# Second MLP product of a token-mixing block: five of seven block products take both parts of their moving operand in one 512-column matmul

## The chip, the cores and the metric

The kernel runs on one core of a Trainium2 chip. The metric is the device time of one execution in microseconds (us). Every time below that carries a position, such as "at 393.73", counts from the start of the profiled span.

## The reference, cut to what matters

Two blocks follow one another on an array x of 2048 tokens by 512 channels: linear attention with a residual, then an MLP over the token axis with a residual. All is float32.

```python
h = x + _A_ref(_layernorm(x), A_wqkv, A_w_phi, A_wo)
# _B_ref on layernorm(h), h here normalised once more:
u = jnp.einsum("bsd,sf->bdf", h, w1) + b1     # f = 1792
u = _gelu(u)
y = jnp.einsum("bdf,fs->bds", u, w2) + b2     # s = 2048
out = h + y transposed to (tokens, channels)
```

The change concerns only the last product, y = u w2.

## The kernel before, in words

**Split products.** Every large product is taken in three matmuls on rounded numbers. An operand is split in a high part (rounded, made by ScalarE) and a low part (the rest, made by VectorE or GpSimd), and the matmuls are high by high, high by low and low by high, summed in PSUM. `split` (L56 to L59) does this: L58 is the ScalarE copy, L59 the subtraction.

**The second MLP product.** The output is made in eight pairs of 128-row blocks (`sp` = 0 to 7), the contraction over f in seven pairs of 128 (`p` = 0 to 6). For each (sp, p) there is a 2 by 2 block product with 256 by 256 blocks of columns, and it is computed in Strassen-Winograd's way: seven block products instead of eight, on sums of blocks of w2 (stationary) and of u (moving). `STEPS` (L775) lists the 56 steps. A stationary block is 128 by 128, a moving block 128 by 256 (`HD`), with its high and low part lying side by side in one tile (`UB[p, m]`, 128 by 2 by 256). So a step is 7 products of 3 matmuls of 256 columns, 21 matmuls (`product`, L799 to L801). All seven sums of a pair of row blocks fit in four PSUM banks of 2 by 256 columns; two sums share a bank. Pairs with even sp take the four banks of pool `ps_b`, pairs with odd sp the two of `ps_f` and the two of `ps_q`, eight banks in all (L818, L819).

**Preparing w2.** `stream_w2` (L779 to L793) prepares two steps at a time, called a group here. It loads the blocks (L785, SyncE's DMA queue), forms three sums and replaces one block by a difference (L789 to L792, VectorE, 128 by 256 each), and splits the 128 by 1792 result (L793, which calls L58 on ScalarE into `whi` and L59 on VectorE into `wlo`). `whi` and `wlo` have two buffers each and `wraw` three, so the split of group g+1 begins when TensorE is done with group g-1. A pair of row blocks is seven steps, so its end falls in the middle of a group after even sp, and on the end of a group after odd sp.

**Closing a pair.** At p = 6 the products are issued bank by bank (L825, L830). Then (L832 to L839) ScalarE copies one sum to SBUF (`e`), VectorE forms `u2`, `u3` and the second `e` from banks and SBUF, and two VectorE operations of 512 columns add the bias and the remaining banks into `ot`. GpSimd's queue then sends two DMAs that add `ot` to the output in memory (L839), where the residual already stands. The last pair (L842 to L859) instead loads its rows of the output to `hb`, collects the last three steps bank by bank, and adds everything there on VectorE.

**What sets the order.** From L709 on, no order is written by hand: a list scheduler with its own estimates of durations fixes the order on each engine at build time. It takes the ready instruction that was traced first. So TensorE's order can differ from the loop's: where a low part is late by the scheduler's estimate, matmuls with high parts are put ahead. On the chip each engine follows the fixed order and waits where it must. A bank counts as one thing: VectorE and ScalarE read it only after all traced matmuls into it.

Of the kernel before, what the change touches and what calls it, by code (L numbers as in the profile page):

```python
# [9 lines left out]
F32 = mybir.dt.float32  # L10
F32R = mybir.dt.float32r
AF = mybir.ActivationFunctionType
ALU = mybir.AluOpType
# [4 lines left out]
P = 128  # L18
# [16 lines left out]
def block_kernel(ctx: ExitStack, tc: tile.TileContext, x, xT, wT, phic, wo, w1, b1, w2, b2,  # L35
                 kvmask, ident_in, out):
    nc = tc.nc
# [9 lines left out]
    b2s = cst.tile([P, NT], F32, name="b2s")  # L47
# [8 lines left out]
    def split(hi, lo, src, lo_engine):  # L56

        nc.scalar.activation(hi, src, AF.Copy)  # L58
        lo_engine.tensor_sub(lo, src, hi)  # L59
# [9 lines left out]
    ps_q = ctx.enter_context(tc.tile_pool(name="ps_q", bufs=2, space=PSUM, side="right"))  # L69
# [28 lines left out]
    def load_x(t):  # L98
        raw = kk.tile([P, KD, P], F32, name="xraw", bufs=3)
        nc.sync.dma_start(raw, xT[t])  # L100
        return raw
# [298 lines left out]
    for t in range(3, NT - 1):  # L400
        if t + 2 < NT:
            raw = load_x(t + 2)
# [108 lines left out]
    ps_f = ctx.enter_context(tc.tile_pool(name="ps_f", bufs=2, space=PSUM, reuse_waits="tile"))  # L511
# [210 lines left out]
    NP = NF // 2  # L722
    HD = D // 2
    up = ctx.enter_context(tc.tile_pool(name="up", bufs=1, side="right", reuse_waits="tile"))
    uo = ctx.enter_context(tc.tile_pool(name="uo", bufs=2, side="right", reuse_waits="tile"))
    ws = ctx.enter_context(tc.tile_pool(name="ws", bufs=2, side="right", reuse_waits="tile"))
    ur = ctx.enter_context(tc.tile_pool(name="ur", bufs=4, side="right", reuse_waits="tile"))
    ut = ctx.enter_context(tc.tile_pool(name="ut", bufs=1, side="right", reuse_waits="tile"))
    ps_b = ctx.enter_context(tc.tile_pool(name="ps_b", bufs=4, space=PSUM, reuse_waits="tile"))
# [3 lines left out]
    U, UB, far = {}, {}, {}  # L733
# [39 lines left out]
    hp = ctx.enter_context(tc.tile_pool(name="hp", bufs=1, reuse_waits="tile"))  # L773

    STEPS = [(sp, p) for sp in range(NT // 2) for p in range(NP)]  # L775
    GRP = 2
    AW = {}

    def stream_w2(n):  # L779
        steps = STEPS[n:n + GRP]  # L780
        raw = ws.tile([P, GRP, 7, P], F32, name="wraw", bufs=3)
        wh_ = ws.tile([P, GRP, 7, P], F32R, name="whi")
        wl_ = ws.tile([P, GRP, 7, P], F32R, name="wlo")
        for i, (sp, p) in enumerate(steps):
            nc.sync.dma_start(raw[:, i, 0:4].rearrange("p (k i) s -> p k (i s)", k=2),  # L785
                              w2v[:, 2 * p:2 * p + 2, sp * 2 * P:(sp + 1) * 2 * P])
            AW[sp, p] = wh_[:, i], wl_[:, i]
        with tc.issue_after(LO[-18]):
            nc.vector.tensor_add(raw[:, :, 4], raw[:, :, 0], raw[:, :, 2])  # L789
            nc.vector.tensor_sub(raw[:, :, 0], raw[:, :, 1], raw[:, :, 0])  # L790
            nc.vector.tensor_sub(raw[:, :, 5], raw[:, :, 4], raw[:, :, 1])
            nc.vector.tensor_sub(raw[:, :, 6], raw[:, :, 3], raw[:, :, 5])  # L792
        split(wh_, wl_, raw, nc.vector)  # L793


    PROD = ((1, 1, 0, 0, True), (2, 6, 2, 1, True), (3, 3, 3, 1, True), (4, 4, 2, 0, False), (0, 0, 1, 0, True),
            (5, 5, 0, 1, False), (6, 2, 3, 0, False))

    def product(o, a, b, start, stop):  # L799
        for i, (x, y) in enumerate(((0, 0), (0, 1), (1, 0))):  # L800
            nc.tensor.matmul(o, a[x], b[:, y], start=start and i == 0, stop=stop and i == 2, skip_group_check=True)  # L801

    def products(sp, ps, order):
        for a, b, bk, half, opens in order:
            for p in ps:
                wh_, wl_ = AW[sp, p]
                product(bank[bk][:, half], (wh_[:, a], wl_[:, a]), UB[p, b], p == 0 and opens, p == NP - 1)

    def flat(a):
        return a.rearrange("p k d -> p (k d)")  # L810

    for n, (sp, p) in enumerate(STEPS):
        t = 2 * sp
        last = t + 2 == NT
        if n % GRP == 0:
            stream_w2(n)
        if p == 0:
            pools = [ps_f, ps_f, ps_q, ps_q] if sp % 2 else [ps_b] * 4  # L818
            bank = [pool.tile([P, 2, HD], F32, name="py", tag="pu") for pool in pools]  # L819
        if p < NP - 1 - 2 * last:  # L820
            products(sp, [p], PROD)
            continue
        if p < NP - 1:
            continue
        by_bank = sorted(PROD, key=lambda m: m[2:4])  # L825
        e = uo.tile([P, 2, HD], F32, name="e")
        u2 = uo.tile([P, HD], F32, name="u2", bufs=1)
        u3 = uo.tile([P, HD], F32, name="u3")
        if not last:
            products(sp, [p], by_bank)  # L830
            ot = uo.tile([P, 2, 2, HD], F32, name="ot", bufs=1)
            nc.scalar.activation(e[:, 1], bank[0][:, 0], AF.Copy)  # L832
            nc.vector.tensor_add(u2, bank[0][:, 1], e[:, 1])
            nc.vector.tensor_add(u3, bank[1][:, 0], u2)
            nc.vector.tensor_add(e[:, 0], bank[2][:, 0], u2)
            for i, add in enumerate((u3.unsqueeze(1).to_broadcast([P, 2, HD]), e)):
                nc.vector.scalar_tensor_tensor(ot[:, i], bank[2 + i], b2s[:, t + i:t + i + 1], add,  # L837
                                               op0=ALU.add, op1=ALU.add)
                nc.gpsimd.dma_start(out[(t + i) * P:(t + i + 1) * P, :], flat(ot[:, i]), accum_op=ALU.add)  # L839
            continue  # L840

        hb = [hp.tile([P, 2, HD], F32, name=f"hb{i}") for i in range(2)]  # L842
        for i in range(2):
            nc.sync.dma_start(flat(hb[i]), out[(t + i) * P:(t + i + 1) * P, :])
            nc.vector.tensor_scalar(hb[i], hb[i], b2s[:, t + i:t + i + 1], None, op0=ALU.add)
        products(sp, [p - 2, p - 1, p], by_bank)
        nc.scalar.activation(e[:, 1], bank[0][:, 0], AF.Copy)
        nc.vector.tensor_add(hb[1][:, 1], bank[0][:, 0], hb[1][:, 1])
        nc.vector.tensor_add(u2, bank[0][:, 1], e[:, 1])
        nc.vector.tensor_add(hb[1][:, 0], u2, hb[1][:, 0])  # L850
        nc.vector.tensor_add(u3, bank[1][:, 0], u2)
        nc.vector.tensor_add(hb[0], hb[0], u3.unsqueeze(1).to_broadcast([P, 2, HD]))
        nc.vector.tensor_add(hb[0][:, 0], bank[2][:, 0], hb[0][:, 0])
        nc.vector.tensor_add(hb[1][:, 0], bank[2][:, 0], hb[1][:, 0])
        nc.vector.tensor_add(hb[0][:, 1], bank[2][:, 1], hb[0][:, 1])
        nc.sync.dma_start(out[t * P:(t + 1) * P, :], flat(hb[0]))
        for k, q in ((0, nc.scalar), (1, nc.sync)):
            nc.vector.tensor_add(hb[1][:, k], bank[3][:, k], hb[1][:, k])
            q.dma_start(out[(t + 1) * P:NT * P, k * HD:(k + 1) * HD], hb[1][:, k])  # L859
# [47 lines left out]
```

## Time and profile before

| what | value |
|---|---|
| median of 3 runs | 526.02 us (525.8 to 526.22) |
| profiled execution, its own time | 526.04 us |
| its span in the trace | 524.3 us |
| second MLP product: first and last matmul start | 378.62 and 519.61 us |
| TensorE busy over the span | 517.7 us, 4000 matmuls |
| VectorE busy | 384.5 us, 681 instructions |
| ScalarE busy | 277.8 us, 475 instructions |
| GpSimd busy | 229.4 us, 174 instructions |

Rows of the profile name a group by the kernel's line, the engine (PE is TensorE, PEld its weight loads, DVE VectorE, ACT ScalarE, POOL GpSimd, SP SyncE), the operation, and the tiles as output<-inputs with their shape. After the bar come the busy time and the mean of one in ns, then the idle time of the engine before these instructions with what ended it. In a timeline the first column is the start, the second how long the row lasts; rows of one kind that follow one another are merged ("x8"). Matmuls are pipelined, so the duration of one (283 ns for 256 columns) is longer than the distance between two starts, and it is the distance that counts.

### The profile page before, as it was taken

How to read it: one execution, taken by the hardware profiler on the slowest of the kernel's cores; microseconds unless marked ns; L12 is line 12 of the kernel's file. 1: busy time of each engine (PE TensorE's matmuls, PEld its weight loads, DVE VectorE, ACT ScalarE, POOL GpSimd, SP SyncE). 2: the span in 40 equal slices, each digit the busy share in tenths (PEclk: the TensorE clock that was granted, in tenths of full speed). 3: DMA queues.
4: the chain of work that ended last, by engine and by line, in shares of the span. 5: the costliest groups of instructions: out<-in, count | busy, mean ns of one | idle time of the engine just before them, and what ended most of it. 6: DMA issues, size and time to landing. Idle time of an engine off the chain costs nothing.

```text
span 524.3 us, 10150 instructions
## 1 busy us (share of the span) xinstructions
PE 517.7 (99%) x4000; PEld 446.6 (85%) x4000; DVE 384.5 (73%) x681; ACT 277.8 (53%) x475; POOL 229.4 (44%) x174
## 2 busy tenths in 40 slices
PE   8999999999999999999999999999999999999996
PEld 7888888887877777777788888888899999999996
DVE  6893999986997899697336425726668878888774
ACT  6999853434267877767756433426544333343330
POOL 2579698985989999974224000000001101101110
PEclk9999999999999999999999999999999999999999
DMA  8643210021303333333255432532015556535631
GB/s 304 198 132 121 75 47 22 1 83 60 103 21 101 102 101 108 115 101 123 81 173 154 115 101 81 181 102 80 20 41 122 144 139 154 126 123 133 150 71 50
DMA packets 45487, 55.85 MB, mean 107 GB/s; under 512 B 3968, under 2 KB 33024, under 8 KB 45440
## 3 DMA queue, kind: packets, MB, share of 16 engines
q1 hardware_dynamic: 43136, 51.38, 30.9%
q0 software_dynamic: 2016, 3.67, 5.3%
q8 instruction: 31, 0.51, 0.4%
q10 hardware_dynamic: 288, 0.17, 0.1%
q14 instruction: 16, 0.13, 0.1%
HBM read 46.81 MB, written 8.39 MB: 105 GB/s over the span
## 4 chain that ended last, share of the span: by engine, by line
PE 95%; DVE 3%; ACT 1%; issue 0%; DVEq 0%; ACTq 0%
PE py L801 26%; PE pu L63 13%; PE pu L64 12%; PE pu L65 12%; PE pv L64 3%; PE pv L65 3%; PE po L63 3%; PE pv L63 3%; PE po L65 3%; PE po L64 3%; PE pk_ps L63 2%; PE pk_ps L65 2%; PE pk_ps L64 2%; PE pn L549 2%; PE tr L531 2%; PE kvp L208 2%
## 5 line engine op out<-in xcount | busy, mean ns | idle before, releaser
L839 POOL DMA_DIRECT2D out<-ot x14 | 12.4, 996 | 210.9 <-DVE ot L837 210.9
L801 PE MATMUL py<-uf,whi 128*128 128x256 f32 x560 | 96.2, 283 | 0.0
L58 ACT ACTIVATE whi<-wraw 128x1792 fp32r<-128x1792 f32 x28 | 47.7, 1704 | 77.9 <-PE py L801 73.8
L63 PE MATMUL pu<-hs,whi 128*128 128x512 f32 x224 | 87.7, 394 | 0.0
L64 PE MATMUL pu<-hs,whi 128*128 128x512 f32 x224 | 87.2, 389 | 0.0
L65 PE MATMUL pu<-hs,wlo 128*128 128x512 f32 x224 | 86.7, 389 | 0.0
L801 PEld LDWEIGHTS py<-uf,whi 128*128 128x128 f32 x560 | 83.3, 192 | 0.0
L610 DVE TENSOR_TENSOR wlo<-wraw,whi 128x512 fp32r<-128x512 f32 x56 | 47.3, 847 | 44.7 <-ACT whi L603 44.5
L59 DVE TENSOR_TENSOR wlo<-wraw,whi 128x1792 fp32r<-128x1792 f32 x28 | 56.6, 2022 | 18.6 <-ACT whi L58 18.6
L801 PE MATMUL py<-uf,wlo 128*128 128x256 f32 x280 | 69.9, 283 | 0.0
L603 ACT ACTIVATE whi<-wraw 128x512 fp32r<-128x512 f32 x56 | 34.6, 625 | 45.0 <-PE pu L64 40.8
L63 PEld LDWEIGHTS pu<-hs,whi 128*128 128x128 f32 x224 | 42.0, 188 | 9.1 <-ACT hj L581 0.2
L801 PEld LDWEIGHTS py<-uf,wlo 128*128 128x128 f32 x280 | 49.7, 192 | 0.0
L65 PEld LDWEIGHTS pu<-hs,wlo 128*128 128x128 f32 x224 | 42.0, 188 | 8.9
L64 PEld LDWEIGHTS pu<-hs,whi 128*128 128x128 f32 x224 | 42.1, 188 | 8.5
L443 POOL TENSOR_TENSOR ez<-eq,zB 128x1024 f32<-128x1024 f32 x16 | 38.5, 2408 | 4.4 <-ACT zB L487 4.4
L801 PE MATMUL py<-un,whi 128*128 128x256 f32 x224 | 38.4, 283 | 0.0
L196 POOL TENSOR_TENSOR pk<-pk,sk 128x1024 f32<-128x1024 f32 x16 | 31.0, 1941 | 7.7 <-DVE sk L195 5.4
L467 POOL TENSOR_TENSOR eq<-eq,w 128x1024 f32<-128x1024 f32 x16 | 32.4, 2025 | 3.2 <-DVE w L464 3.2
L801 PEld LDWEIGHTS py<-un,whi 128*128 128x128 f32 x224 | 33.2, 192 | 0.1
L200 POOL TENSOR_TENSOR zacc<-zacc,pk 128x1024 f32<-128x1024 f32 x13 | 31.2, 2404 | 0.5
L172 ACT ACTIVATE pk<-pk,r 128x1024 f32<-128x1024 f32 x16 | 18.4, 1147 | 17.9 <-DVE pk L150 17.7
(172 smaller groups left out, 1174.6 us busy)
## 6 DMA issues: line engine op xcount, KB each, us to landing
wraw<-in_w SPq DMA_DIRECT2D x112, 256.0 KB, 2.9
xraw<-in_xT SPq DMA_DIRECT2D x16, 256.0 KB, 3.1
xh<-in_x SPq DMA_DIRECT2D x16, 256.0 KB, 2.6
h<-in_x SPq DMA_DIRECT2D x16, 256.0 KB, 2.7
out<-h SPq DMA_DIRECT2D x16, 256.0 KB, 2.0
out<-ot POOLq DMA_DIRECT2D x14, 256.0 KB, 4.7
wraw<-in_wT SPq DMA_DIRECT2D x12, 256.0 KB, 5.1
wo<-in_wo SPq DMA_DIRECT2D x4, 256.0 KB, 3.8
```

The costliest lines, as they stand in the source:

```text
L58: nc.scalar.activation(hi, src, AF.Copy)
L59: lo_engine.tensor_sub(lo, src, hi)
L63: nc.tensor.matmul(o, ah, bh, start=first, stop=False)
L64: nc.tensor.matmul(o, ah, bl, start=False, stop=False)
L65: nc.tensor.matmul(o, al, bh, start=False, stop=last)
L196: nc.gpsimd.tensor_mul(heads(PK[t]), heads(PK[t]), sk.unsqueeze(2).to_broadcast([P, 2 * H, DH]))
L200: nc.gpsimd.tensor_add(zacc, zacc, PK[t])
L443: nc.gpsimd.tensor_mul(EZ[t], EQ[t], zB)
L467: nc.gpsimd.tensor_mul(heads(EQ[t]), heads(EQ[t]), W[t].rearrange("p g c h -> p (g c h)").unsqueeze(2).to_broadcast([P, 2 * H, DH]))
L603: nc.scalar.activation(wh_, raw, AF.Copy)
L610: LO.append(nc.vector.tensor_sub(wl_, raw, wh_).ins)
L801: nc.tensor.matmul(o, a[x], b[:, y], start=start and i == 0, stop=stop and i == 2, skip_group_check=True)
```

## The change

For pairs sp = 0 to 6, five of the seven products become "wide": one matmul of 512 columns takes the high stationary part against high and low moving part at once, and a second one of 256 columns takes the low stationary part against the high moving part. The 512 results are a full bank: the high sums in one half, the low sums in the other. These five products have a bank each (`b3`, `b2`, `b7`, `b5`, `b4`). The other two (P1 and P6) stay as they were and share `b16`. A pair now takes six banks: `b3` and `b2` come from `ps_f` and `ps_q` in turn, and `b16`, `b7`, `b5`, `b4` are the four banks of `ps_b` in every pair. At p = 0 to 5 the order is b3, b2, then b16, b7, b5, b4; at p = 6 it is b16, b7, b5, b4, then b3, b2.

Closing a pair now has six ScalarE copies of 256 columns (the `e` of before and the five low halves into `low`), seven VectorE operations of 256 columns (three as before, and four in the place of two of 512), and four GpSimd additions (three of 512 columns, one of 256) that bring `low` into `ot` before each DMA. `in_order` ties these ScalarE and VectorE operations to one order within each engine.

The last pair keeps its 21 narrow matmuls per step, in an order by bank at all p, and takes its four banks from `ps_b`. The split of w2 does the low part in two VectorE operations of 896 columns, one per step. The last group's `whi` and `wlo` get buffers of their own.

```diff
+        end = n + GRP == len(STEPS)
+        wh_ = (hp if end else ws).tile([P, GRP, 7, P], F32R, name="whi")
+        wl_ = (hp if end else ws).tile([P, GRP, 7, P], F32R, name="wlo")
...
-        split(wh_, wl_, raw, nc.vector)
+        nc.scalar.activation(wh_, raw, AF.Copy)
+        for i in range(GRP):
+            nc.vector.tensor_sub(wl_[:, i], raw[:, i], wh_[:, i])
...
+    P1, P2, P3, P4, P5, P6, P7 = (1, 1), (3, 3), (6, 2), (2, 6), (4, 4), (5, 5), (0, 0)
+
+    def narrow(o, ps, m, sp, opens, closes):
+        for p in ps:
+            wh_, wl_ = AW[sp, p]
+            for i, (x, y) in enumerate(((wh_, 0), (wh_, 1), (wl_, 0))):
+                nc.tensor.matmul(o, x[:, m[0]], UB[p, m[1]][:, y], start=opens and p == 0 and i == 0,
+                                 stop=closes and p == NP - 1 and i == 2, skip_group_check=True)
+
+    def wide(o, p, m, sp):
+        wh_, wl_ = AW[sp, p]
+        nc.tensor.matmul(o, wh_[:, m[0]], UB[p, m[1]], start=p == 0, stop=False, skip_group_check=True)
+        nc.tensor.matmul(o[:, 0], wl_[:, m[0]], UB[p, m[1]][:, 0], start=False, stop=p == NP - 1, skip_group_check=True)
+
+    def in_order(*groups):
+        at = {}
+        for op in [op for group in groups for op in group]:
+            with ExitStack() as st:
+                for ins in at.values():
+                    st.enter_context(tc.issue_after(ins))
+                ins = op().ins
+            at[ins.engine] = ins
...
+        if not last:
+            if p == 0:
+                b3, b2 = [new_bank((ps_f, ps_q)[sp % 2]) for _ in range(2)]
+                b16, b7, b5, b4 = [new_bank(ps_b) for _ in range(4)]
+            first, second = ([lambda: wide(b3, p, P3, sp), lambda: wide(b2, p, P2, sp)],
+                             [lambda: narrow(b16[:, 0], [p], P1, sp, True, True),
+                              lambda: narrow(b16[:, 1], [p], P6, sp, False, True),
+                              lambda: wide(b7, p, P7, sp), lambda: wide(b5, p, P5, sp), lambda: wide(b4, p, P4, sp)])
+            for f in second + first if p == NP - 1 else first + second:
+                f()
...
+            low = hp.tile([P, 5, HD], F32, name="low")
+            copies = [lambda: nc.scalar.activation(e[:, 1], b16[:, 0], AF.Copy)]
+            for i, o in ((0, b5), (4, b7), (1, b4), (2, b3), (3, b2)):
+                copies.append(lambda i=i, o=o: nc.scalar.activation(low[:, i], o[:, 1], AF.Copy))
+            adds = [lambda: nc.vector.tensor_add(u2, b16[:, 1], e[:, 1]),
+                    lambda: nc.vector.tensor_add(u3, b7[:, 0], u2),
+                    lambda: nc.vector.tensor_add(e[:, 0], b5[:, 0], u2)]
+            for i, k, o, add in ((0, 0, b5, u3), (0, 1, b4, u3), (1, 0, b3, e[:, 0]), (1, 1, b2, e[:, 1])):
+                adds.append(lambda i=i, k=k, o=o, add=add: nc.vector.scalar_tensor_tensor(
+                    ot[:, i, k], o[:, 0], b2s[:, t + i:t + i + 1], add, op0=ALU.add, op1=ALU.add))
+            in_order(copies[:1] + adds[:1], adds[1:2], copies[1:4], adds[2:5], copies[4:], adds[5:])
+            nc.gpsimd.tensor_add(ot[:, 0], ot[:, 0], low[:, 0:2])
+            nc.gpsimd.tensor_add(ot[:, 0], ot[:, 0], low[:, 4:5].to_broadcast([P, 2, HD]))
+            nc.gpsimd.dma_start(out[t * P:(t + 1) * P, :], flat(ot[:, 0]), accum_op=ALU.add)
+            nc.gpsimd.tensor_add(ot[:, 1], ot[:, 1], low[:, 2:4])
+            nc.gpsimd.tensor_add(ot[:, 1, 0], ot[:, 1, 0], low[:, 0])
+            nc.gpsimd.dma_start(out[(t + 1) * P:(t + 2) * P, :], flat(ot[:, 1]), accum_op=ALU.add)
+            continue
         if p == 0:
-            pools = [ps_f, ps_f, ps_q, ps_q] if sp % 2 else [ps_b] * 4
+            b16, b7, b54, b32 = [new_bank(ps_b) for _ in range(4)]
...
+        if p < NP - 3:
+            for o, m, opens in places:
+                narrow(o, [p], m, sp, opens, True)
```

More of the change, by code (lines that the diff above doesn't have):

```diff
@@ L781, in stream_w2 @@
         raw = ws.tile([P, GRP, 7, P], F32, name="wraw", bufs=3)
-        wh_ = ws.tile([P, GRP, 7, P], F32R, name="whi")
-        wl_ = ws.tile([P, GRP, 7, P], F32R, name="wlo")
+        end = n + GRP == len(STEPS)
+        wh_ = (hp if end else ws).tile([P, GRP, 7, P], F32R, name="whi")
+        wl_ = (hp if end else ws).tile([P, GRP, 7, P], F32R, name="wlo")
         for i, (sp, p) in enumerate(steps):
@@ L792, in stream_w2, with new_bank @@
             nc.vector.tensor_sub(raw[:, :, 6], raw[:, :, 3], raw[:, :, 5])
-        split(wh_, wl_, raw, nc.vector)
[L796 to L807, printed above, removed]
+        nc.scalar.activation(wh_, raw, AF.Copy)
[20 more added lines that the diff above has]
+            at[ins.engine] = ins
     def flat(a):
         return a.rearrange("p k d -> p (k d)")
+    def new_bank(pool):
+        return pool.tile([P, 2, HD], F32, name="py", tag="pu")
     for n, (sp, p) in enumerate(STEPS):
@@ L816, in block_kernel @@
             stream_w2(n)
-        if p == 0:
-            pools = [ps_f, ps_f, ps_q, ps_q] if sp % 2 else [ps_b] * 4
-            bank = [pool.tile([P, 2, HD], F32, name="py", tag="pu") for pool in pools]
-        if p < NP - 1 - 2 * last:
-            products(sp, [p], PROD)
+        if not last:
[8 more added lines that the diff above has]
+                f()
+            if p < NP - 1:
+                continue
+            e = uo.tile([P, 2, HD], F32, name="e")
+            u2 = uo.tile([P, HD], F32, name="u2", bufs=1)
+            u3 = uo.tile([P, HD], F32, name="u3")
+            ot = uo.tile([P, 2, 2, HD], F32, name="ot", bufs=1)
+            low = hp.tile([P, 5, HD], F32, name="low")
[15 more added lines that the diff above has]
+            nc.gpsimd.dma_start(out[(t + 1) * P:(t + 2) * P, :], flat(ot[:, 1]), accum_op=ALU.add)
+            continue
@@ L822, in block_kernel @@
+        if p == 0:
+            b16, b7, b54, b32 = [new_bank(ps_b) for _ in range(4)]
+            places = ((b16[:, 0], P1, True), (b16[:, 1], P6, False), (b7[:, 0], P7, True), (b54[:, 0], P5, True),
+                      (b54[:, 1], P4, False), (b32[:, 0], P3, True), (b32[:, 1], P2, False))
+        if p < NP - 3:
+            for o, m, opens in places:
+                narrow(o, [p], m, sp, opens, True)
             continue
         if p < NP - 1:
-            continue
-        by_bank = sorted(PROD, key=lambda m: m[2:4])
@@ L826, in block_kernel @@
[L826 to L839, printed above, removed]
@@ L845, in block_kernel @@
             nc.vector.tensor_scalar(hb[i], hb[i], b2s[:, t + i:t + i + 1], None, op0=ALU.add)
-        products(sp, [p - 2, p - 1, p], by_bank)
+        for o, m, opens in places:
+            narrow(o, [p - 2, p - 1, p], m, sp, opens, True)
+        bank = b16, b7, b54, b32
+        e = uo.tile([P, 2, HD], F32, name="e")
+        u2 = uo.tile([P, HD], F32, name="u2", bufs=1)
+        u3 = uo.tile([P, HD], F32, name="u3")
         nc.scalar.activation(e[:, 1], bank[0][:, 0], AF.Copy)
```

## The prediction

> **What bounds the kernel now.** I read the chain that ended last first, then the matmul starts in the timeline, then the groups and the stage table, and last the waits.
>
> The chain, in order of time; its last rows:
>
> ```profile
> 378.78 137.53 PE py L801 x1146
> 516.33 0.39 ACT e L847
> ...
> 520.55 0.33 DVE hb L858
> ```
>
> The second MLP product is one unbroken run of matmuls. From 516.33 on, the chain leaves TensorE: the closing of the last pair hangs on one ScalarE copy and the VectorE additions behind it. The granted clock is 1.00 in every stretch that I asked for.
>
> The price of a matmul is the distance between starts, at 512 columns (first MLP product) and at 256:
>
> ```profile
> 309.71 0.39 PE L65 MATMUL pu<-hs,wlo 128*128 128x512 f32 x1
> ...
> 317.87 0.39 PE L65 MATMUL pu<-hs,wlo 128*128 128x512 f32 x1
> 380.29 0.28 PE L801 MATMUL py<-un,wlo 128*128 128x256 f32 x1
> 380.41 0.40 PE L801 MATMUL py<-un,whi 128*128 128x256 f32 x2
> 380.65 0.28 PE L801 MATMUL py<-un,wlo 128*128 128x256 f32 x1
> ```
>
> Between the first two rows lie 36 starts: 8.16/36 = 0.2267 us each. The narrow ones start 0.12 apart, and the whole product agrees: (519.61 - 378.62)/1175 = 0.1200. So there is no hole in it, and twice the columns cost 0.1067 more: a matmul is 0.1067 us per 256 columns plus 13.3 ns fixed.
>
> VectorE is the second engine. Groups, and the stage table for 400 to 500 (columns after the stretch: length, then busy time of PE, PEld, DVE, ACT, POOL):
>
> ```profile
> L59 DVE TENSOR_TENSOR wlo<-wraw,whi 128x1792 fp32r<-128x1792 f32 x28 | 56.6, 2022 | 18.6 <-ACT whi L58 18.6
> L790 DVE TENSOR_TENSOR wraw<-wraw 128x256 f32<-128x256 f32 x28 | 11.8, 421 | 0.6
> L837 DVE SCALAR_TENSOR_TENSOR ot<-py,b2s,u 128x512 f32<-128x512 f32 x7 | 5.2, 742 | 0.0
> 400.00:420.00 20.00, 20.00 (x169) 20.00 (x168) 17.45 (x27) 7.04 (x6) 3.69 (x4) 1.00 0.61 129
> 420.00:440.00 20.00, 20.00 (x169) 20.00 (x168) 16.04 (x25) 7.05 (x6) 1.74 (x2) 1.00 0.49 129
> ```
>
> With 15.60, 16.23 and 16.98 in the next three stretches VectorE is busy 82.3 of 100 us, or 14.5 of the 17.64 us (147 x 0.12) of a pair of row blocks. GpSimd does next to nothing here. That changes.
>
> **1. Matmuls: -3.27 us.** A wide product replaces three narrow matmuls (0.360) by one of 512 and one of 256 (0.2267 + 0.12 = 0.3467). Five per step: 0.0667 us; 7 steps in 7 pairs: 49 x 0.0667 = 3.27 us, all on the path. A pair then takes 7 x (5 x 0.3467 + 6 x 0.12) = 17.17 us. The bounds are 0 (a 512 matmul costs two of 256) and 3.27; I take 3.27, the row of 512 being the very form.
>
> [...]
>
> **2. The end: -0.2 us.** Before, the `whi` of the last group waits for a buffer, so the first bank of the last pair closes at 516.3, and ten VectorE operations in a row reach to 520.88. With its own buffers that split can come earlier and the bank closes sooner. What is late next is the last bank: its last matmul starts at 519.61, and a reader starts some 0.3 later, 519.9 instead of L858's 520.13. Bounds 0 and 0.4 (an earlier DMA of the first rows); I take 0.2.
>
> **3. VectorE and GpSimd: 0 to +2.0 us, taken +0.6.** Per pair VectorE has 14 operations L789 to L792, 7 halves of `wlo` (896 columns; between 0.69 us for 512, L610, and 2.02 for 1792: 1.09) and 7 closing operations of 0.42: 5.88 + 7.63 + 2.94 = 16.45 us. Queued ones start 0.33 apart where they last 0.42 (413.33, 413.66), so 28 x 0.08 comes off: 14.2 us packed tight. New are four GpSimd additions per pair: 512 columns with two full inputs are 1.30 us (L59 on POOL), 256 are 0.74 (L745): 4.64 us. They cost VectorE something:
>
> ```profile
> 227.80 1.94 POOL L467 TENSOR_TENSOR eq<-eq,w 128x1024 f32<-128x1024 f32 x1 [1.86 <-DVE w L464]
> 228.19 2.10 DVE L610 TENSOR_TENSOR wlo<-wraw,whi 128x512 fp32r<-128x512 f32 x1
> 234.77 1.94 POOL L467 TENSOR_TENSOR eq<-eq,w 128x1024 f32<-128x1024 f32 x1 [0.43 <-DVE w L464]
> 235.22 2.03 DVE L610 TENSOR_TENSOR wlo<-wraw,whi 128x512 fp32r<-128x512 f32 x1
> ```
>
> An L610 lasts 0.69 alone. Started under a GpSimd operation it ends 0.55 and 0.54 us after that one's end (229.74 to 230.29, 236.71 to 237.25): it stood still until then. L789 to L792 and `wlo` read two SBUF tiles as L610 does; closing operations read a bank. So a pair's additions can hold VectorE for 4.64, less 0.84 for the two closing operations that run beside the first, less 4 x 0.14 (0.69 - 0.55) that passes in the shadow: 3.2 us. 14.2 + 3.2 = 17.4, 0.28 over TensorE's 17.17: +2.0 us in seven pairs if nothing of it falls in idle time. But VectorE idles 3.1 us a pair now, mostly for `whi` (18.6 in L59's row), and part falls there: I take 0.6, nearer to zero. The extra five ScalarE copies (0.385 each, L832) meet an engine that is busy 7 of 20 us. GpSimd has 4.64 us and two DMA issues of 1.0 us in 17: its DMAs land some 5 us later, before `ot` is wanted again.
>
> [...]
>
> **4. Banks: 0 to +6.1 us, taken +1.0.** Before, a pair had four banks that the next did not touch. Now `ps_b` serves every pair, so the next pair's first matmul into `b16` waits for `u2` (its reader), which waits for `e`. Call T the start of step p = 6. TensorE reaches the new `b16` at T + 2.45 (the step) + 0.69 (the new b3 and b2) = T + 3.15. In the trace of before, after an even pair:
>
> ```profile
> 395.55 2.02 DVE L59 TENSOR_TENSOR wlo<-wraw,whi 128x1792 fp32r<-128x1792 f32 x1 [1.42 <-ACT whi L58]
> 395.85 0.38 ACT L832 ACTIVATE e<-py 128x256 f32<-128x256 f32 x1 [0.34 <-PE py L801]
> 397.82 0.42 DVE L833 TENSOR_TENSOR u<-py,e 128x256 f32<-128x256 f32 x1
> ```
>
> T is 393.73; `u2` stands behind a whole `wlo` and ends at 398.24, T + 4.51, 1.36 us too late. After an odd pair it ends at 413.41 with T = 411.37, T + 2.04: in time. Queued behind a waiting b16 matmul is everything on TensorE, unless the scheduler has put the b3 and b2 products of the group's further steps ahead: four wide ones, 1.39 us, just the cover. Halved, `wlo` lets `u2` in 0.93 us earlier. The last pair has no b3 and b2 of its own: its first matmul is due at T + 2.45, so 2.06 us late at before's offsets, some 1.1 with the halves. Upper bound 3 x 1.36 + 2.06 = 6.1; lower bound 0, all covered. I take 0.1 for each of three even pairs and 0.7 for the last: 1.0.
>
> **The sum**, against the profiled execution's own 526.04 (span 524.3 and 1.7 around it; the median is 526.02): 526.04 - 3.27 - 0.2 + 0.6 + 1.0 = 524.2 us.
>
> **Rivals.**
> - *VectorE becomes the bound, and the kernel is slower.* Its work of a pair is then not 14.2 but half way to the 15.3 that today's busy time gives (14.5 + 0.56 for the halves + 0.2 for four closing operations), 14.8, and the whole 3.2 of GpSimd's additions lies on it: 18.0 per pair against 17.64 before. +0.36 x 7 = 2.5, + 1.0 - 0.2: 529.3 us. It decides from 2.8 us held per pair. For it: the four rows above and the backlog of `wlo` just behind a closing. Against it: 3.1 us of idle time.
> - *The banks eat the gain.* Half of the upper bound of step 4, 3.05: 526.04 - 3.47 + 0.6 + 3.05 = 526.2 us. For it: `u2` behind `wlo` in every even pair. Against it: the cover of 1.39.
> - *The 512 matmul saves nothing here*, the fixed 13.3 ns going with each half bank written: 526.04 - 0.2 + 1.6 = 527.4 us. Against it: the 512-column rows write whole banks at 226.7.
>
> **Chances.** The forecast's case 0.56, VectorE 0.21, banks 0.18, no saving 0.05. A measurement can tell about 0.2%, 1.05 us, from no change. Faster: 0.53 of the first and 0.03 of the banks' case, 0.56. Within: 0.03 and 0.10, 0.13. Slower: 0.21, 0.05 of banks, 0.05: 0.31. The forecast's own range is 522.3 (no waits, the end's 0.4) to 525.5. To hold 8 in 10 it has to reach over the banks and half of VectorE's case: 522.3 to 529.3.
>
> **What would show it.** Step 1: wide starts 0.227 and 0.120 apart, a pair of 17.17 us. Step 2: the last pair's `e` copy well before the last bank. Step 3: `wlo` halves of over 1.1 us under a GpSimd addition, and weight loads or matmuls with `wlo` that wait for VectorE. Step 4: idle time before the first b16 matmul of a pair, largest before the last pair. I am wrong if pairs take over 17.64 us, by whichever of these waits.

## The result, and the profile after

The changed kernel takes **554.48 us** (553.44 to 556.48, 6 runs) against 526.13 (525.8 to 526.39, 6 runs with the three above): ratio 1.0545, 95% interval 1.0521 to 1.0569. That is 5.4% slower, 25 us above the top of the predicted range. The profiled execution has a span of 551.7 us, 27.4 more than before. The second MLP product alone went from 141.0 to 169.4 us between its first and last matmul start, 28.4 more; the first MLP product and what lies before it end within 0.4 us of where they ended. All ratios are of undisturbed executions; one execution of the kernel of experiment 6 took 1018.94 us, with TensorE busy for 1011.5 us on its 3755 matmuls (515.3 in experiment 12), for a cause that stays open, and is left out.

Groups of the changed kernel's page. L812 and L813 are the 512-column and the 256-column matmul of a wide product, L796 a half of `wlo`, L790 the first of the four operations on `wraw`:

```profile
L796 DVE TENSOR_TENSOR wlo<-wraw,whi 128x896 fp32r<-128x896 f32 x56 | 61.7, 1152 | 8.8 <-ACT whi L794 8.8
L812 PE MATMUL py<-uf,whi 128*128 128x512 f32 x175 | 57.0, 400 | 5.9 <-ACT whi L794 5.9
L813 PE MATMUL py<-uf,wlo 128*128 128x256 f32 x175 | 37.9, 286 | 7.3 <-DVE wlo L796 7.2
L790 DVE TENSOR_TENSOR wraw<-wraw 128x256 f32<-128x256 f32 x28 | 15.1, 546 | 22.3 <-DMA wraw<-in_w 22.1
```

TensorE, which never waited in this product before, now does, for three things (all its waits in this stage):

```profile
PE py L813 <- DVE wlo L796: 9.1, 9, 1.4
PE py L812 <- ACT whi L794: 5.9, 6, 1.0
PE py L806 <- DVE u L857: 5.4, 6, 3.5
```

These count idle time only. Measured as the distance between two starts beyond 120 ns (256 columns) or 227 ns (512), it is 11.6 us at low parts, 6.9 at high parts and 6.3 at banks that `u2` has yet to read. Of the 31.6 us by which the starts lie further apart than these pitches, that is 24.8; the half clock below takes 2.8, and the rest is in delays of under 0.2 us and in the pitch of the wide matmuls. A pair shows the first two waits behind its closing; timeline of TensorE, then of GpSimd, VectorE and ScalarE in the same stretch:

```profile
403.06 0.28 PE L813 MATMUL py<-uf,wlo 128*128 128x256 f32 x1
404.29 0.73 PE L812 MATMUL py<-uf,whi 128*128 128x512 f32 x2 [0.96 <-ACT whi L794]
...
405.10 0.86 PE L812 MATMUL py<-uf,whi 128*128 128x512 f32 x3
407.35 0.51 PE L813 MATMUL py<-uf,wlo 128*128 128x256 f32 x2 [1.40 <-DVE wlo L796]
```

```profile
402.64 1.39 POOL L867 TENSOR_TENSOR ot<-ot,low 128x512 f32<-128x512 f32 x1 [1.15 <-DVE ot L861]
404.00 1.48 POOL L865 TENSOR_TENSOR ot<-ot,low 128x512 f32<-128x512 f32 x1
402.82 1.50 DVE L792 TENSOR_TENSOR wraw<-wraw 128x256 f32<-128x256 f32 x1
404.36 1.41 DVE L793 TENSOR_TENSOR wraw<-wraw 128x256 f32<-128x256 f32 x1
402.54 3.29 ACT L794 ACTIVATE whi<-wraw 128x1792 fp32r<-128x1792 f32 x2 [2.61 <-PE py L812]
```

L792 and L793 last 0.42 us alone; here they take 1.50 and 1.41 us and end some 0.3 us after a GpSimd addition does (404.32 after 404.03, 405.77 after 405.48), and the `wlo` behind them starts 1.4 us after `whi` was there. ScalarE makes two `whi` in one go: both buffers came free at nearly the same time.

VectorE's waits for the loads of w2 grow too, from 8.0 to 21.2 us in this product, but they are not the price: experiment 12 below still has 17.4 us of them and takes no longer than the kernel before.

The largest single hole (a stretch in which TensorE idles) stands before the last pair, and the clock falls behind it (timeline of TensorE, then the stage table, whose third column from the right is the granted clock):

```profile
522.87 0.76 PE L813 MATMUL py<-uf,wlo 128*128 128x256 f32 x5
527.15 0.80 PE L806 MATMUL py<-un,whi 128*128 128x256 f32 x2 [3.52 <-DVE u L857]
```

```profile
528.00:534.00 6.00, 6.00 (x32) 6.00 (x32) 5.37 (x9) 2.79 (x5) 4.37 (x3) 0.56 0.01 3
534.00:540.00 6.00, 6.00 (x51) 5.94 (x50) 3.28 (x3) 1.71 (x1) 3.49 (x4) 1.00 0.52 70
```

Up to 533.5 the narrow matmuls start 214 ns apart instead of 120: 2.8 us more, on top of the hole's 3.7.

### The profile page after: what moved, and what is told of

It reads as the page before. It is cut to its first block, busy times and chain, and to the rows that moved or that the text cites. A ratio compares the mean times of both kernels' runs of the same rounds, so it can differ in the third digit from the quotient of the medians.

```text
span 551.7 us, 9807 instructions
## 1 busy us (share of the span) xinstructions
PE 524.7 (95%) x3755; PEld 434.4 (79%) x3755; DVE 407.9 (74%) x723; ACT 287.5 (52%) x510; POOL 265.2 (48%) x202
## 5 line engine op out<-in xcount | busy, mean ns | idle before, releaser
L864 POOL TENSOR_TENSOR ot<-ot,low 128x512 f32<-128x512 f32 x7 | 9.0, 1287 | 201.0 <-DVE ot L861 201.0
L796 DVE TENSOR_TENSOR wlo<-wraw,whi 128x896 fp32r<-128x896 f32 x56 | 61.7, 1152 | 8.8 <-ACT whi L794 8.8
L812 PE MATMUL py<-uf,whi 128*128 128x512 f32 x175 | 57.0, 400 | 5.9 <-ACT whi L794 5.9
L813 PE MATMUL py<-uf,wlo 128*128 128x256 f32 x175 | 37.9, 286 | 7.3 <-DVE wlo L796 7.2
L806 PE MATMUL py<-uf,whi 128*128 128x256 f32 x210 | 40.7, 285 | 0.0
L813 PEld LDWEIGHTS py<-uf,wlo 128*128 128x128 f32 x175 | 29.0, 190 | 12.1 <-DVE wlo L796 10.8
L812 PEld LDWEIGHTS py<-uf,whi 128*128 128x128 f32 x175 | 29.6, 189 | 11.1 <-ACT whi L794 7.8
L806 PEld LDWEIGHTS py<-uf,whi 128*128 128x128 f32 x210 | 34.4, 194 | 2.3
L790 DVE TENSOR_TENSOR wraw<-wraw 128x256 f32<-128x256 f32 x28 | 15.1, 546 | 22.3 <-DMA wraw<-in_w 22.1
```

Of the source, the lines that this page charges most:

```text
L796: nc.vector.tensor_sub(wl_[:, i], raw[:, i], wh_[:, i])
L806: nc.tensor.matmul(o, x[:, m[0]], UB[p, m[1]][:, y], start=opens and p == 0 and i == 0, stop=closes and p == NP - 1 and i == 2, skip_group ...
L812: nc.tensor.matmul(o, wh_[:, m[0]], UB[p, m[1]], start=p == 0, stop=False, skip_group_check=True)
L813: nc.tensor.matmul(o[:, 0], wl_[:, m[0]], UB[p, m[1]][:, 0], start=False, stop=p == NP - 1, skip_group_check=True)
```

## The experiments

Three theories are named in what was expected. A hand-over is the step from one pair's closing to the next pair's first use of the same banks. **L**: GpSimd's additions hold VectorE, so `wlo` comes late. **B**: two buffers of `whi` and `wlo` are too few once TensorE runs products of later steps early, since both then stay in use and the next split starts late. **S**: sharing `ps_b` between pairs is the price.

**1. The changed kernel without GpSimd's additions**

```diff
-            nc.gpsimd.tensor_add(ot[:, 0], ot[:, 0], low[:, 0:2])
-            nc.gpsimd.tensor_add(ot[:, 0], ot[:, 0], low[:, 4:5].to_broadcast([P, 2, HD]))
...
-            nc.gpsimd.tensor_add(ot[:, 1], ot[:, 1], low[:, 2:4])
-            nc.gpsimd.tensor_add(ot[:, 1, 0], ot[:, 1, 0], low[:, 0])
```

> The changed kernel without its four GpSimd additions per pair; the low sums of the wide products are copied to SBUF but left out of the output. The order on TensorE is the same for the first half of the product. Theory L (the additions hold VectorE, so wlo comes late): VectorE gets back some 3.4 us per pair, the wlo waits of TensorE (9 to 13 us in all) go, and the time falls below 542. Theory B (products pulled ahead keep both whi/wlo buffers taken, so the next split starts too late): whi waits of about 1.1 us per pair stay, the time stays above 545.

Measured: 535.58 us, ratio to before 1.019 (1.0175 to 1.0205), 18.9 us less than the changed kernel. The waits for `wlo` fall from 11.6 to 0.4 us, measured as distances, and the other losses fall with them: waits for `whi` from 6.9 to 5.1, for `u2` from 6.3 to 3.3, the loss at half clock from 2.8 to 1.5 (granted clock 0.91 from 500 to 520). The waits that are left, in idle time:

```profile
PE py L812 <- ACT whi L794: 4.2, 6, 1.0
PE py L806 <- DVE u L857: 2.8, 3, 2.5
```

The operations on `wraw` are back at 0.42 us each. Over the product VectorE's L790 to L793 and L796 take 21.3 us less, 3.0 per pair, so the hold itself was predicted well (3.2). L is right for the largest part; most of the `whi` waits stay, as B says, though the time fell far below B's 545.

**2. A third pair of `whi` and `wlo` tiles**

```diff
-        end = n + GRP == len(STEPS)
+        end = n > 0 and n // GRP % 3 == 0
```

> The changed kernel with a third whi and wlo buffer (every third group takes the pair of tiles that only the last group had). Theory B: the split of the next group no longer waits for TensorE; whi and wlo waits go and the time falls below 535. Theory L: VectorE is held as before, so at most the whi waits (7 us) go: about 547.

Measured: 548.16 us, 1.0413 (1.0377 to 1.0449), 6.3 us less than the changed kernel. In its profiled execution (544.46 us, the fastest of four) no wait for `whi` is left; those for `wlo` are 9.0 us and for `u2` 7.4. That is near L's forecast for this edit, and it sizes B's part.

**3. The kernel before with one set of banks**

```diff
-            pools = [ps_f, ps_f, ps_q, ps_q] if sp % 2 else [ps_b] * 4
+            pools = [ps_b] * 4
```

> The kernel before with one edit: every pair takes the four banks of ps_b. No wide products, no additions. Theory S (sharing banks between pairs is the price): at least +1.5 us per hand-over, over 535. Theories L and B: TensorE's work is unchanged and little is late, 526 to 531.

Measured: 546.13 us, 1.0392 (1.0368 to 1.0416). Sharing alone, with no wide matmul and no addition, costs 20 us, far beyond the 6.1 that the prediction held for the most. The first hand-over in its timeline:

```profile
395.14 2.02 DVE L59 TENSOR_TENSOR wlo<-wraw,whi 128x1792 fp32r<-128x1792 f32 x1 [1.43 <-ACT whi L58]
395.73 0.28 PE L801 MATMUL py<-uf,wlo 128*128 128x256 f32 x1
397.42 0.42 DVE L833 TENSOR_TENSOR u<-py,e 128x256 f32<-128x256 f32 x1
397.89 0.73 PE L801 MATMUL py<-un,whi 128*128 128x256 f32 x2 [1.89 <-DVE u L833]
```

It is the picture of step 4: `u2` stands behind a whole `wlo`, here with no b3 and b2 to cover it. The seven waits for `u2` are 10.2 us; four waits for `wlo` add 3.2. After the four longest of the seven the clock falls, which costs 5.8 us and which the prediction had not priced at all:

```profile
398.00:400.00 2.00, 2.00 (x10) 2.00 (x11) 2.00 (x6) 0.00 (x0) 0.00 (x0) 0.50 0.78 253
```

**4. The kernel before with GpSimd's additions alone** (of a tile of zeros; same diff as in 1, with the other sign)

> The kernel before with the four GpSimd additions per pair put in (of a tile of zeros, so the output is as before). The order on TensorE is the same as before's. Theory L: 4.6 us of additions per pair hold VectorE for some 3.4 us, and TensorE waits for wlo: 530 to 545. Theories B and S: GpSimd is off the path, 526 to 527.

Measured: 537.55 us, 1.022 (1.0203 to 1.0237). TensorE's order is before's; all its waits are for `wlo`, 9.4 us at nine places, and one half-clock stage follows (1.5 us; granted clock 0.91 from 420 to 440). L holds with neither a wide matmul nor a shared bank.

**5. As 1, with TensorE in the traced order** (the step loop put under `tc.manual_schedule(engines={ET.PE})`)

> The kernel of the first experiment (GpSimd additions out, low sums left out of the output) with TensorE's instructions kept in the order in which the loop traces them, so that no product of a later step is put ahead. Theory B (pulling ahead is what keeps both buffers taken): the whi waits of 5.1 us go, and the time falls from 535.6 to about 531 or below. Theory S (the shared banks are the price, and pulling ahead pays part of it): the waits for u2 grow by more than that, to 538 or more.

Measured: 552.25 us, 1.047 (1.043 to 1.0511), 16.7 slower than experiment 1. Its `whi` waits are gone, as B says, but S's forecast holds: TensorE waits 18 us, measured as distances, for the closing of the shared banks, and stages at half clock take 6.1 more (mean granted clock 0.988). Those waits in idle time:

```profile
PE py L806 <- DVE u L859: 6.1, 4, 2.0
PE py L812 <- DVE ot L863: 5.8, 3, 2.1
PE py L812 <- ACT low L858: 3.0, 6, 0.6
```

So running ahead is no fault of the order. It covers the hand-over of the banks, and pays for that with buffers of `whi` and `wlo`, of which two don't suffice.

**6. As 1, with the third pair of tiles** (run twice; the trace is the second run's)

> The kernel of the first experiment with a third pair of whi and wlo tiles. Theory B: the whi waits (5.1 us) go and nothing takes their place: about 530. Theory S: TensorE then stands at the shared banks instead, waits for u2 grow from 3.3 us, and the time stays at 534 or above.

> The kernel without GpSimd additions and with the third pair of tiles once more, for a trace of an undisturbed execution (low sums left out of the output). Theory B plus L: TensorE waits for neither whi nor wlo; what stays is at most 2 us at shared banks, and wide matmuls at about 235 ns instead of 227: 526 to 531.

Measured: 529.01 us, 1.0042 (1.0021 to 1.0063), and 529.23 the second time; TensorE waits for `whi` and `wlo` nowhere. One hole of 2.7 us is left, before the last pair, with a half-clock stage behind it (mean granted clock 0.996).

**7. The split of w2 alone** (halves of `wlo` and own tiles for the last group, on the kernel before)

> The kernel before with only the two small parts of the change: wlo in two halves, and tiles of its own for the last group. All theories: within 1 us of 526; the end up to 0.4 us shorter. If it is slower by more than 2 us, the other order that the scheduler then gives TensorE is a cause of its own that none of the theories has.

Measured: 525.63 us, 0.999 (0.9981 to 0.9999). From the last matmul start to the end of the span it takes 4.24 us instead of 4.66: step 2, 0.4 instead of 0.2.

**8. P7 alone wide, in the bank whose other half was empty**

```diff
+                if bk == 1 and sp < NT // 2 - 1:
+                    nc.tensor.matmul(bank[1], wh_[:, a], UB[p, b], start=p == 0, stop=False, skip_group_check=True)
+                    nc.tensor.matmul(bank[1][:, 0], wl_[:, a], UB[p, b][:, 0], start=False, stop=p == NP - 1, skip_group_check=True)
+                    continue
...
+            nc.vector.tensor_add(u3, bank[1][:, 1], u3)
```

> The kernel before with one wide product, P7, which has a bank of its own there already (its other half is empty), so that no bank is shared with the next pair and GpSimd has nothing to do; VectorE adds the low sum, one more operation of 0.42 us per pair. Where the wide matmul is sound by itself: 49 products save 7 ns each at the pitch that the changed kernel's trace shows (235 and 118 ns against three of 120), 0.3 us, or 13 ns each at the pitch that was predicted, 0.65 us: 525.1 to 525.8. If the wide form carries a cost that was not seen, over 527.

Measured: 525.52 us, 0.9985 (0.9976 to 0.9994). A wide product is sound by itself; TensorE does not wait once, and the product is 0.70 us shorter: 14 ns for each of the 49 wide products, all that step 1 promised.

**9. Experiments 7 and 8 together**

> The two parts of the change that were harmless alone, put together on the kernel before: P7 wide in its own bank, wlo in halves and tiles of its own for the last group. No bank is shared and GpSimd adds nothing. If the two gains add: about 0.6 + 0.5 us less than before, 525.0. If VectorE's extra operations (one per pair, one per group) or the new order make something late: 525.5 to 526.5.

Measured: 525.36 us, 0.999 (0.9981 to 0.9999). The gains do not add; its tail is 4.63 us, so the end's 0.4 is given back. Whether that comes from the order that the scheduler makes is not shown.

**10. The changed kernel with the third pair of tiles and the additions on VectorE** (`nc.vector.tensor_add` for `nc.gpsimd.tensor_add`)

> The changed kernel with the third pair of tiles and with its four additions per pair on VectorE instead of GpSimd, so nothing is left out of the output. Theory L (the price is that a GpSimd addition stops VectorE for as long as it runs, 4.6 us per pair, where the same additions cost VectorE itself some 2.3 us): well under the 548.2 of the kernel with the third pair and GpSimd additions, 531 to 538. If the price is the additions as such, wherever they stand: 543 or more.

Measured: 539.85 us, 1.0265 (1.0231 to 1.0299), 8.3 less than with GpSimd's additions (experiment 2) and 10.8 more than with none. Between the two forecasts: the additions cost VectorE time wherever they stand, and on GpSimd they cost nearly twice as much (548.16 less 529.01, 19.2 us).

**11. The changed kernel, two of the last pair's banks from `ps_q`**

```diff
-            b16, b7, b54, b32 = [new_bank(ps_b) for _ in range(4)]
+            b16, b7, b54, b32 = [new_bank(pool) for pool in (ps_q, ps_q, ps_b, ps_b)]
```

> The changed kernel with one edit: the last pair takes two of its four banks from ps_q, which stand empty, and only two from ps_b. Theory S for the last pair: the hole of 3.7 us before its first matmul goes, and with it the 6.8 us at half clock that follow it (about 3 us lost): 547 to 550. If other waits simply take its place: 552 or more.

Measured: 555.61 us, 1.0561 (1.0539 to 1.0582): the second forecast. The hole before the last pair is gone, and another has come later:

```profile
538.75 0.43 PE L806 MATMUL py<-uf,wlo 128*128 128x256 f32 x1 [3.01 <-DVE wlo L796]
```

While GpSimd's additions of the pair before ran (531.59 to 537.75), the four halves of `wlo` took from 532.92 to 539.69. With VectorE that late, the last pair's banks are not what ends last.

**12. All three edits: no additions, the third pair, the last pair's banks**

> Without GpSimd additions, with the third pair of tiles, and with two of the last pair's banks from ps_q (low sums left out of the output). The kernel with the first two edits still had one hole of 2.7 us before the last pair's first matmul and a stage of 3.4 us at half clock behind it. Theory S for the last pair: with wlo no longer late both go, some 4.4 us: 523.5 to 525.5, and the saving of the wide matmuls (1.7 to 3.3 us) is seen at last. If another wait takes the hole's place again, as in the changed kernel: 528 or more.

Measured: 524.03 us, 0.9967 (0.9954 to 0.998). The granted clock stays at 1.00, and 1.0 us of waits is left. With the edits of experiments 1, 2 and 11 together the saving of the wide matmuls is seen at last, but the low sums are missing from this output.

**13. The same on the full kernel, with the low sums added by DMA**

```diff
+            for dst, src in ((rows[0], flat(ot[:, 0])), (rows[1], flat(ot[:, 1])), (rows[0], flat(low[:, 0:2])),
+                             (rows[1], flat(low[:, 2:4])), (rows[0][:, 0:HD], low[:, 4]), (rows[1][:, 0:HD], low[:, 0]),
+                             (rows[0][:, HD:D], low[:, 4])):
+                nc.gpsimd.dma_start(dst, src, accum_op=ALU.add)
```

> The same two edits on the full kernel, with the low sums brought in by adding DMAs from GpSimd's queue (five more per pair, nothing left out of the output) instead of by GpSimd additions. If GpSimd's price is the additions' hold on VectorE, and DMA issues (about 1 us each) do not hold it: no waits for wlo, 524 to 527. If DMA issues hold VectorE too, or the chains of additions to one row of the output keep the low sums' tile taken until the next pair wants it: 530 or more.

Measured: 551.65 us, 1.051 (1.0438 to 1.0583). The second forecast: the DMAs to one row of the output wait for one another, 4.2 to 5.2 us each from issue to landing, and the tile of low sums is still taken when ScalarE wants it for the next pair. The loads of w2 also land later, 5.1 us after issue instead of the 3.3 of experiment 12. From the waits:

```profile
DVE wraw L790 <- DMA wraw<-in_w: 26.7, 12, 4.3
POOL out L868 <- DMA out<-low: 24.4, 14, 3.9
ACT low L856 <- DMA out<-low: 21.4, 5, 8.1
```

## Why the prediction was wrong

- **Step 1 (matmuls, -3.27 us): right in kind, mis-sized by a third.** A 512 matmul of a wide product starts the next one after 235 ns (median), not 227; in experiment 12 the 244 distances are 8.1 ns longer on average, 2.0 us, and the narrow ones give 0.9 back. That leaves some 2.2 us. In experiment 8 the 512 matmul takes 235 ns too, but there the narrow matmuls give all of it back. Why 235 here and 227 in the first MLP product was not tried.
- **Step 2 (the end): right**, 0.4 instead of 0.2 in experiment 7.
- **Step 3 (VectorE and GpSimd, +0.6, at most +2.0): this step failed.** The hold was sized well: 3.0 us per pair against 3.2, or 21.3 in all. Its price was not: taking the additions out saves 18.9 us (experiment 1), and putting them into the kernel before costs 11.8 (experiment 4). I added up VectorE's work of a whole pair and set it against TensorE's 17.17 us, as if the hold could move to where VectorE idles. It can't: the additions start when a pair closes, and in the same few us the next `wlo` falls due. Idle time elsewhere in the pair is of no use to it, and TensorE, which had no hole to spare, doesn't make one up.
- **Step 4 (banks, +1.0, at most +6.1): failed too.** Sharing the banks alone costs 20.4 us (experiment 3). I had the hand-over after an even pair right: before's offsets gave 2.06 us too late without b3 and b2, and the wait at 397.89 adds 2.04. I held odd pairs to be in time, and they wait up to 1.07. And I took the cover by the next steps' b3 and b2 as free. The cover holds `whi` and `wlo` of two groups in use, so that the splits come in pairs and late (experiments 2, 5, 6): 6.3 to 6.6 us. The last pair, which has no cover, was taken at 0.7: its hole is 3.7 us in the changed kernel, and without the additions still 2.7 (experiment 6).
- **Not priced at all: the clock.** Stages at half clock behind holes cost 2.8 us in the changed kernel and 5.8 in experiment 3.
- **The rival "VectorE becomes the bound"** named the mechanism and the right side, and gave 529.3: it too worked with the sum of a pair. *The banks eat the gain* named the other part, and its 3.05 us left out the cover's price and the clock. *The 512 matmul saves nothing here* is refuted by experiments 8 and 12.

The account in runs: from 554.48, the additions are 18.9 us; the third pair of tiles takes 6.6 more (529.01 less 535.58); the last pair's banks 5.0 (524.03 less 529.01); and 1.7 us below before (0.9967) is what the wide matmuls and the end had to give. Of the 5.0, 3.3 lie in the product: the hole and the half clock behind it. The other 1.6 lie behind its last matmul, where the end takes 5.70 us in experiment 6, 4.10 in experiments 1 and 12: in experiment 6 the last pair's first bank is read only 2.2 us before the last matmul starts. The parts are not independent: the third edit alone gave nothing (experiment 11), the second alone 6.3. No version with the whole output beats the kernel before by more than 0.15%: that is experiment 8.

## What to carry to other kernels

Price a delay on a second engine against the due time of what is queued behind it, not against that engine's idle time over a stage; the idle time counts only if it lies between the delay and the due time. Freeing a few ns per instruction on the bounding engine is worth little when it takes a double buffer (here of PSUM banks) away: try first the one piece that needs no new buffer, as P7 did. Where a scheduler may run work ahead to cover a wait, count the buffers which that work holds.

## What the runs showed of the hardware

- A hole's length alone did not decide whether the clock fell. Holes of 2.04 to 2.11 us were followed by a stage of 3.41 us at half clock, four times out of four in experiment 3 (the first: granted clock 0.50 from 398 to 400, 0.65 from 400 to 402); in experiment 4 a hole of 2.01 us was, and one of 1.97 us was not; in experiment 2 one of 2.58 us was, and one of 3.49 us was not. Behind the 3.7 us of the changed kernel the granted clock was 0.50 from 526.45 to 533.28.
- Within a trace the stages start whole multiples of 3.413 us apart: in experiment 3 at 398.00, 438.96, 479.92 and 520.88, 12 x 3.413 = 40.96 each; in the changed kernel at 526.45 and, behind the last matmul, at 550.35, 7 x 3.413 = 23.89. Cut the traces of this product that have such stages (the changed kernel and experiments 1 to 6, 10, 11 and 13) at such distances from their stages, and add up in each stretch of 3.413 us what the starts lie apart beyond 120 or 235 ns. Of 432 stretches at full clock, all 17 with 2.04 us or more were followed by half clock, none of the 407 under 1.95 us was, and of the 8 between them 3 were. In the changed kernel one of 49 holds 2.98 us, with half clock behind it, and the others 1.66 at most. The hole of 3.49 us in experiment 2 lies across the border of two stretches, 517.86: they idle 1.96 and 1.63 us. In experiment 5 a hole of 1.50 and one of 0.60 us with two short delays made 2.3 us in one stretch, and half clock followed at 486.54. So in these traces half clock went with the idle time in a stretch, not with the length of one hole.
- In the changed kernel a VectorE operation with two SBUF inputs that began while GpSimd added two SBUF tiles took longer: the six such L793 1.40 us instead of 0.42, with their end 0.3 us after the addition's, and the five such halves of `wlo` 1.61 to 2.17 us instead of 1.09. Operations that read a bank did not: the eight L861 beside an addition took 0.48 us, as without. GpSimd's additions took longer too: the one from 532.11 on, with a half of `wlo` already under way, 2.13 us, where the first addition of a pair takes 1.29 on average; in experiment 4 the second addition of a pair takes 3.07 on average, where the first, of the same shape, takes 1.29. DMA issues of GpSimd (0.9 us each on average, experiment 13) did not stretch VectorE's operations: 0.42 us on `wraw` and 1.09 for a half of `wlo` there, and 0.42 and 1.08 for those beside an issue in the changed kernel.
